# New fixed orders of four engines in the first part of an adaLN, linear-attention and MLP kernel

## The chip, the cores and the metric

The kernel runs on one core of a Trainium2 chip. The metric is the device time of one execution in microseconds (us). The program is written in the Tile layer of the chip's kernel language: a planner places tiles and semaphores, and each engine runs its own queue of instructions in order. The engines are named as in the profile: PE (TensorE, matrix products; its weight loads are shown as PEld), DVE (VectorE), ACT (ScalarE), POOL (GpSimd) and SP (SyncE, whose queue issues nearly all DMA transfers).

## What is computed

x is 2048 x 576, all float32. Six vectors of length 576 (sa, ca, ga, sb, cb, gb) come from the condition c.

```
mod = silu(c) @ w_mod, cut into sa, ca, ga, sb, cb, gb
h = layernorm(x) * (1 + ca) + sa
q, k, v = split(h @ wqkv)                  # 32 heads of 18
pq, pk = phi(q), phi(k)                    # phi(t) = (t + 1 if t > 0 else exp(t)) + 1e-6
kv = sum over s of pk v;  z = sum over s of pk
o = (pq kv) / (pq z + 1e-6)
x = x + ga * (o @ wo)
h = layernorm(x) * (1 + cb) + sb
x = x + gb * (silu(h @ w1) @ w2)           # w1: 576 x 4608, w2: 4608 x 576
```

## The kernel before

Every product is made of three passes: each float32 operand is split into a high part and a low remainder in the matrix unit's rounded float32 form (fp32r), and high by high, high by low and low by high are summed in psum. The high part is a cast, mostly on ACT (`split_h` L201, `w_hi` L294, the fetch of MLP weights L921 and L969); the low part is a subtraction, mostly on DVE (L117, and `w_lo` L299/L301).

The work has three parts.

1. *The front and attention* (0 to about 350 us). LayerNorm statistics (`stats` L174/175, `finish` L179 to L181, `normalise` L187/189), the modulation vectors (`add_mod`, `col_mod` L346, products with w_mod by L496/L498 on DVE from raw loads L263), transposes, and then k, v, kv and z for each of 16 tiles of 128 rows; later q, num and den, and the product with wo (`attn_out`, whose last step L737 adds a psum result to the residual tile `acc`, on DVE). At the very start PE runs products of ones by ones (`warm_up`, L395), 8 and then 10 in number, each two records of PE in the profile. The raw tiles of wqkv are loaded into parts of the `acc` tiles, which hold the residual later.
2. *The first MLP block beside attention* (from about 215 us). While the last tiles of attention are worked, a first group of the MLP is computed with its own tiles: `mlp_up` (L797, silu L799), `mlp_down` (L808 into the psum buffer `big`, added to `acc` by L813). The normalised tokens h of the second LayerNorm are transposed and stored to DRAM (`hd`, stores L873) on SP.
3. *The MLP* (from about 390 us to the end). Seven products of a Strassen-like scheme, with h streamed from `hd` (fetch L987/L991). `Unit.up` (L1233) and `Unit.down` (L1306) are PE's products; DVE adds the results (L1252, L1314). Weights come by `Weights.load1` (w1: a main transfer of 512 KB at L953 and two tails of 64 KB at L955) and `Weights.load2` (w2: 576 KB at L962) into tiles `v`. A w2 tile is multiplied by gb first (L918: one operation on DVE, two halves on POOL), sums of w1 pieces are made on POOL (L936 to L948), and a tail is cast to `wtb` on ACT (L921) with its low part on DVE (L117).

Two tiles `v` of the third part are the ones that held attention's merged matrix (`big<-v` of L222 on PE, one of attention's last products), so their first loads wait until PE has read it for the last time.

What sets the order: PE runs in the order of the program's text. For DVE, ACT, POOL and SP the first part and the second have fixed orders that are written out by hand: `ORDERS` (L55 to L99) holds for each engine a permutation of the numbers of its instructions (DVE 545, ACT 373, POOL 127, SP 109), and `arrange` makes each instruction follow the one listed before it on its engine. From the third MLP unit on, all engines run in program order. An instruction that waits holds up everything behind it on its engine.

Of the kernel before, what the change touches and what calls it, by code (L numbers as in the profile page):

```python
# [22 lines left out]
def kernel(ctx: ExitStack, tc, A_x, A_wqkv, A_wo, B_x, B_w1, B_w2, c, w_mod, out):  # L23
# [28 lines left out]
    def f32(ap):  # L52
# [1 line left out]

    ORDERS = {  # L55
        "DVE": """
            4 1 0 3 2 5-7 13 8 14 12 10 15 9 11 16-21 25-26 31 27 32 28 33-34 22-23 35 24 41-44 30 29 39 36-38 45-46
            40 47 50 48-49 62-63 65 51-52 56 66 84 64 57 53 55 58 61 85 59 86 80 60 88 81 87 67 83 68 82 69 71 70 72
            148 73-74 89 75-77 149 91 78 90 79 150 92 151 54 93 97 94 98 96 152 100 153 99 95 101-105 107 106
            108-109 111 110 125-126 128-129 127 131 130 132 134 133 135-137 112 138-139 113 141 140 114-115 142  # L60
            116-124 143-147 182-183 154 184-185 158 155 186 159 187 156 160 223 161-162 157 224-225 222 163 226 165
            164 166-171 173 172 192-193 195-196 194 197-199 201-202 200 203-204 174 205 208 175 209 176-177 206-207
            178-180 188 181 189-191 210-214 216 215 217-218 220 219 221 227-228 230-231 229 232-248 250-251 249
            252-254 256-258 255 259 261 263 260 265-266 262 264 269-271 275 268 276 267 277 273 272 274 300 282-284
            278-279 291-293 280 299 303-305 285 312-313 301 286-287 281 288 302 289 314 294 290 322 295-296 323
            297-298 324 306 331-332 307-310 315 333 341 311 316-319 342 320 325 343 321 353-354 326-329 334 355 330
            365 335 366 336-337 367 374 338 375 346 339 344-345 351 347 340 348-349 376 352 357-358 350 359-361 356
            385 362 386 363-364 387 368 404-405 369-371 406 372 423 373 377-378 424 379-380 383 382 381 391 388 390
            425 393 432 394-395 398 400 397 384 433 409-410 396 411-413 392 414 420 434 389 401 421 403 426 415 422
            399 427-428 431 417 402 416 407 429 418-419 430 435 408 436-437 440 438 441 444 504 439 442-443 446-450  # L70
            445 451 454 452-453 456-460 455 462 461 463 472 475 465 464 479 466 476 474 467 480 478 473 484 468-469
            481 471 486-487 470 482 492 494 493 495 489 488 496 483 497-498 490 499 502 477 491 500 485 503 501 520
            516 508 538 505 507 506 519 511 510 509 515 514 512-513 517-518 521 524 522-523 527 537 525-526 530-531
            529 532-535 528 536 539-544
        """,
        "Activation": """
            0-2 4-5 8 6-7 12 9 13 10-11 22 14 17 19 21 23-25 15-16 18 26-27 29 3 20 35 30 28 37-38 31 33 32 55-56
            58-59 36 39 57 42 44 40 45 41 43 50 53 51 34 54 52 60 46 48 47 61 49 62 64-67 63 69 68 70-74 76-77 75 78
            81 79 82 80 83 94-95 92 84 93 85-91 96-100 103-104 101 105 108 106 109 107 102 110-113 115-116 114 117
            120 118 121 119 122 131 133 123 134 124 132 125-130 135-138 140-141 139 142 145 143 146 144 147-149  # L80
            151-152 150 153 156 154 157 155 158-179 181 180 182-183 185 184 186-191 204 192-194 203 195 198 196-197
            205 199 202 200-201 206-207 210 208-209 219 216 213-214 212 218 211 217 215 220 223 221-222 224 226 228
            227 231 230 232 225 229 233-235 238 236-237 247 242 241 248 239 243 245 249-250 246 251 240 244 252-255
            259 261 257 260 256 262 264-265 263 273 267 266 258 269-270 278-279 268 282 280-281 277 275 274 276 283
            271-272 284-286 288 290-291 287 289 292 297-298 295 294 296 293 316 313 299 301-302 318 300 315 319-320
            317 303 305 304 307-308 314 309-310 306 311 322 312 323 328-329 325 324 321 330-331 326-327 333 332 334
            362 349 344 335-337 340 338 346 343 341 339 345 347 342 351 348 353 359 352 350 354 356 360 358 357 363
            361 365 364 355 366-370 372 371
        """,
        "Pool": """  # L90
            6 0 4 3 2 5 7-15 20 16-17 19 18 21-23 25 24 26 33 27 30 28 34 31-32 29 37 41 35-36 38-39 44 47 42-43 50
            45 40 54 46 48-49 57 51-52 60 84 55-56 53 72 58-59 76 61 79 62-64 73-74 67-68 77 65 78 71 66 69 75 80-81
            70 100 99 82-83 94 89-92 85-87 93 88 102 104 98 97 96 95 101 105-106 103 107-108 113 109-110 112 120 111
            114 117 122 115 119 118 123 121 124 116 125-127
        """,
        "SP": """
            0-26 28 27 29 36 30-31 37-40 45-47 32-35 48-51 53 52 54 41-44 61 60 59 55-57 62 58 63-67 70 68 71 69
            72-74 82 80 76-77 75 83 78 90 79 81 85 87 86 84 88 104 103 89 91 102 92 95 93 96 94 97-101 105 108
            106-107  # L99
        """,  # L100
    }

# [251 lines left out]
    def add_mod(k0, k1):  # L354

        o = sums[:, :, k0 * P : min(k1 * P, D)]
        V.scalar_tensor_tensor(o, mods[3][:, :, k0 * P : min(k1 * P, D)], sc[:, 3:4], o, op0=ALU.mult, op1=ALU.add)
        if k1 > KC:
            A.copy(sums[:, :, D:DX], sums[:, :, KC * P : D])

    def col_mod(k0, k1):
        for k in range(k0, k1):
            for a in range(2):
                mod_mm(sums[:, a], k, ones, a, last=True)
        V.tensor_add(cols["a"][:, k0:k1, :], mod_slots[k0 >= HEAD][:, :, :, 0],
                     plus1.unsqueeze(1).to_broadcast([P, k1 - k0, 2]))
# [17 lines left out]
    def k_part(tiles, passes, first=False, last=False):  # L384
        for n, (a, b) in enumerate(passes):
            for i in tiles:
                for h in range(2):
                    T.matmul(kps[i][:, h, :HALF], hT[0][:, a, i * P : i * P + P], wk_(b)[:, h * HALF : (h + 1) * HALF],
                             start=first and n == 0, stop=last and n == len(passes) - 1)
# [3 lines left out]
    def warm_up(n):  # L393
        for _ in range(n):
            T.matmul(warm_ps[:, 0, 0:P], ones, ones, start=True, stop=True)  # L395

    with tc.manual_schedule(engines={mybir.EngineType.PE}):
# [40 lines left out]
        def first_k(k):  # L438
            k_part(range(2), [(k, k), (KC + k, k)], k == 0)
# [6 lines left out]
        modulate(*args[1], A)  # L446
        add_mod(HEAD, KC + 1)
        ln.stats(2, xts[2])
        first_k(0)
        col_mod(HEAD, KC + 1)  # L450
        turn_tiles(pT, (0, 1), (KC,))
# [1050 lines left out]
```

## Time and profile before

| | us |
|---|---|
| median of 3 runs | 1165.44 |
| lowest and highest of them | 1164.58 and 1167.25 |
| the profiled execution, its own time | 1165.17 |
| its span in the trace | 1163.2 |
| PE busy | 1137.3 (98%) |
| DVE busy | 972.7 (84%) |
| POOL busy | 646.6 (56%) |
| ACT busy | 532.1 (46%) |

The span runs from the first to the last instruction in the trace; the execution's own time is 2.0 us longer. The mean granted clock of PE is 0.992 of full speed. The page of the profile sums the busy time by engine, cuts the span into 40 slices, follows back the chain of work that ended last and groups the instructions by line and operation. The trace answers further: a list of what each engine waited for, timelines of one engine, and windows (busy time of each engine in a stretch with the granted clock of PE and the share in which DMA was busy). An entry of a timeline is the start in us, the duration in us, the engine, the line, the operation, the tiles (out<-in) and the form; xN means N instructions in a row, and the bracket gives the idle time before and the instruction that ended it.

### The profile page before, as it was taken

The page shows a single profiled execution, that of the slowest core. Times are in us where ns is not written, and L with a number is a line of the kernel's source. Part 1 is how long each engine was busy: PE and PEld are TensorE (multiplying, and loading weights), DVE is VectorE, ACT ScalarE, POOL GpSimd, SP SyncE. Part 2 cuts the span into 40 slices and gives each one's busy share as a digit, 9 for nine tenths or more (in the row PEclk, how much of TensorE's full clock was granted, in tenths as well). Part 3 has the DMA queues.
Part 4 walks back from the last instruction along what each step waited for, and adds up shares of the span by engine and source line. Part 5 has one row for each costly group of instructions (what it writes and reads, how often), then busy time and mean ns, then how long its engine had stood idle before and what let it go on. Part 6 is the DMA issues. An engine that isn't in the chain of part 4 may idle for free.

```text
span 1163.2 us, 19621 instructions
## 1 busy us (share of the span) xinstructions
PE 1137.3 (98%) x7239; PEld 1058.0 (91%) x7239; DVE 972.7 (84%) x1552; ACT 532.1 (46%) x1087; POOL 646.6 (56%) x742
## 2 busy tenths in 40 slices
PE   8999999999996899999999999999999999999998
PEld 7999999899995799999999999999999999999998
DVE  5975643587767889999999999999999999999996
ACT  4643442436554444444454454444444444444541
POOL 1100000353624477677767757767766776776686
PEclk8999999999998999999999999999999999999999
DMA  9522100123238869769779788797697797697784
GB/s 291 149 80 76 43 1 1 47 69 122 65 123 314 292 263 348 277 259 366 270 266 351 263 304 321 259 339 294 252 352 278 258 349 278 257 365 266 265 309 153
DMA packets 57231, 268.62 MB, mean 231 GB/s; under 512 B 5484, under 2 KB 19312, under 8 KB 34096
## 3 DMA queue, kind: packets, MB, share of 16 engines
q1 hardware_dynamic: 57124, 267.36, 62.9%
q8 instruction: 58, 0.95, 0.3%
q14 instruction: 37, 0.30, 0.1%
q10 hardware_dynamic: 12, 0.00, 0.0%
HBM read 250.56 MB, written 16.78 MB: 230 GB/s over the span
## 4 chain that ended last, share of the span: by engine, by line
PE 93%; DMA 2%; DVE 2%; ACT 1%; issue 1%; POOL 0%; SPq 0%; DVEq 0%; ACTq 0%; POOLq 0%
PE up L1233 33%; PE down L1306 31%; PE psK L222 13%; PE big L222 7%; PE kvp L547 2%; PE big L808 2%; PE small L797 1%; DMA acc<-in_A_wqkv_dram 1%; PE big L723 1%; PE small L210 1%; DMA hT<-in_w_mod_dram 1%; DVE hT L117 1%; PE psT L210 1%; PE up L1336 1%; PE down L1336 1%; PE psK L691 1%
## 5 line engine op out<-in xcount | busy, mean ns | idle before, releaser
L1314 DVE TENSOR_TENSOR acc<-down,acc 128x576 f32<-128x576 f32 x330 | 246.1, 753 | 14.2 <-PE down L1306 5.2
L1233 PE MATMUL up<-hT,w 128*128 128x512 f32 x916 | 239.4, 390 | 0.8 <-DVE f L1252 0.8
L1233 PEld LDWEIGHTS up<-hT,w 128*128 128x128 f32 x916 | 164.5, 188 | 25.8 <-DVE f L1252 1.2
L1268 POOL TENSOR_TENSOR s<-f,f 128x256 f32<-128x256 f32 x66 | 51.8, 784 | 158.8 <-ACT f L1249 158.7
L1306 PE MATMUL down<-w,hb 128*128 128x288 f32 x792 | 120.8, 294 | 0.0
L1306 PE MATMUL down<-w,hc 128*128 128x288 f32 x792 | 120.6, 294 | 0.0
L1306 PEld LDWEIGHTS down<-w,hb 128*128 128x128 f32 x792 | 113.8, 188 | 5.3 <-DVE hb L1287 0.2
L1306 PEld LDWEIGHTS down<-w,hc 128*128 128x128 f32 x792 | 113.8, 188 | 5.1
L1314 DVE TENSOR_TENSOR U<-down,U 128x576 f32<-128x576 f32 x132 | 99.5, 754 | 17.4 <-PE down L1306 15.3
L117 DVE TENSOR_TENSOR w<-v,w 128x288 fp32r<-128x288 f32 (+1 forms) x170 | 113.2, 675 | 1.0 <-ACT w L977 0.9
L222 PE MATMUL psK<-w,hT 128*128 128x288 f32 (+2 forms) x660 | 107.8, 298 | 0.0
L222 PEld LDWEIGHTS psK<-w,hT 128*128 128x128 f32 x660 | 94.9, 189 | 0.3 <-DVE a L315 0.2
L1233 PE MATMUL up<-room,w 128*128 128x512 f32 x348 | 91.1, 390 | 0.0
L1287 POOL TENSOR_TENSOR hc<-s,hc 128x512 fp32r<-128x512 f32 x66 | 89.2, 1351 | 1.5 <-ACT hc L1283 1.5
L1249 ACT ACTIVATE f<-f 128x512 f32<-128x512 f32 x102 | 64.4, 632 | 47.9 <-DVE f L1254 25.5
L1252 DVE TENSOR_TENSOR f<-up,p 128x512 f32<-128x512 f32 x102 | 69.7, 683 | 14.0 <-PE up L1233 12.1
L180 POOL TENSOR_TENSOR rstd<-ve,neghalf 128x4 f32<-128x4 f32 (+3 forms) x10 | 9.7, 966 | 120.7 <-DVE ve L179 110.7
L1233 PEld LDWEIGHTS up<-room,w 128*128 128x128 f32 x348 | 62.5, 188 | 9.6 <-DMA room<-hd 0.2
L1272 POOL TENSOR_TENSOR f<-f,s 128x256 f32<-128x256 f32 x66 | 50.7, 768 | 36.9 <-DVE hb L1287 26.2
L977 ACT CAST w<-v 128x288 fp32r<-128x288 f32 x85 | 36.7, 434 | 74.6 <-PE down L1306 61.6
L1306 PE MATMUL down<-w,ha 128*128 128x288 f32 x396 | 63.0, 294 | 0.0
L1306 PE MATMUL down<-w,hd 128*128 128x288 f32 x396 | 62.9, 294 | 0.0
(285 smaller groups left out, 2534.8 us busy)
## 6 DMA issues: line engine op xcount, KB each, us to landing
hT<-hd SPq DMA_DIRECT2D x66, 1280.0 KB, 5.9
hT<-hd SPq DMA_DIRECT2D x45, 1024.0 KB, 5.6
room<-hd SPq DMA_DIRECT2D x35, 1280.0 KB, 5.9
room<-hd SPq DMA_DIRECT2D x20, 1024.0 KB, 5.0
v<-in_B_w_dram SPq DMA_DIRECT2D x17, 576.0 KB, 6.5
v<-in_B_w_dram SPq DMA_DIRECT2D x17, 512.0 KB, 8.4
hd<-S SPq DMA_DIRECT2D x6, 1024.0 KB, 8.3
xt<-in_A_x_dram SPq DMA_DIRECT2D x16, 288.0 KB, 4.6
```

What stands on the lines that cost most here:

```text
L117: return V.tensor_sub(lo, full, f32(hi))
L210: T.transpose(ps[:, i * P : (i + 1) * P], xt[i][:, cidx * P : (cidx + 1) * P], ident)
L222: T.matmul(ps, xpart(a), wpart(b), start=n == 0, stop=n == len(XW) - 1)
L977: A.copy(self.w2[n][:, 0], src)
L1233: T.matmul(ps, left, right, start=first and m == 0, stop=m == len(seq) - 1, skip_group_check=True)
L1249: A.activation(self.f[i, k], self.f[i, k], AF.Silu)
L1252: V.tensor_add(f, self.bank[bank[1]], self.p1)
L1268: G.tensor_add(self.s[:, 0:1], half(i, 0, 1), half(i, 1, 1))
L1272: G.tensor_sub(half(i, 1, 0), half(i, 1, 0), self.s[:, 1:2])
L1287: eng.tensor_sub(t[:, :, 1, :], src, f32(t[:, :, 0, :]))
L1306: T.matmul(ps[:, p, :HALF], self.a[i, n][:, u, p * P : (p + 1) * P], self.w.w2[n][:, v], start=n in (1, 5, 7, 6) and j == 0, stop=j == 2, ...
L1314: V.tensor_add(dst, ps[:, :, :HALF], dst)
```

## The change

Two things are changed. First, all four lists in `ORDERS` are new permutations of the same numbers. Second, one line is added: `warm_up(8)`, eight more products of ones by ones, 16 records of PE, behind the statistics of the third token tile and ahead of the first products with wk. The rest of PE's order is unchanged. Since the new lists take three lines fewer and the call one more, lines behind L443 have a number smaller by two in the kernel after, and those ahead of it by three.

What moves, by the lines of the code before:

- ACT at the start: before w cast 0 (L294), w cast 1, h of the first half tile (L201), L195, a normalise, h of the second, w 2, w 3, w 4, three normalises, L195, h of the third and fourth, three more w casts, a load of the activation table with one small operation (L414), h of the fifth. After: w 0, h of the first, L195, w 1, h of the second, the table load with its operation, w 2, w 3, a normalise, w 4, three normalises, a cast of wv, L195, h of the third, then the other casts and h in turn.
- SP near 350 us: before, the load of w2 (L962, number 90) stood ahead of stores of h (L873, numbers 79 and 81) and of the loads of w1 (L955 and L953, numbers 85 to 87). After: the stores first (79, 78, 81, 84), then the two tails (87, 86), the main part (85), then L962 (90).
- DVE near 350 us: before, L918 (number 504) stood ahead of two of the last three additions of attention (L737, the first of them number 446). After: it stands behind all of them, behind the normalise of the last tile (L189) and behind the low part of `wtb` and of the first w pieces. The low part of `wtb` (number 472) stands ahead of the last normalise.
- POOL near 350 us: the two halves of L918 (numbers 100 and 99) stood ahead of the sums of w1; after, they stand behind them.
- Elsewhere neighbours change places on DVE, ACT and POOL, among them the L498 products with the later pieces of w_mod between 45 and 62 us.

The diff, cut to its core:

```diff
     ORDERS = {
         "DVE": """
...
-            445 451 454 452-453 456-460 455 462 461 463 472 475 465 464 479 466 476 474 467 480 478 473 484 468-469
+            440 442 444 441 443 446-447 439 448-449 454 450 455 451-453 445 456-459 464 460 472 463 461 478 462 504
...
-            425 393 432 394-395 398 400 397 384 433 409-410 396 411-413 392 414 420 434 389 401 421 403 426 415 422
-            399 427-428 431 417 402 416 407 429 418-419 430 435 408 436-437 440 438 441 444 504 439 442-443 446-450
...
         "Activation": """
-            0-2 4-5 8 6-7 12 9 13 10-11 22 14 17 19 21 23-25 15-16 18 26-27 29 3 20 35 30 28 37-38 31 33 32 55-56
+            0-2 4 6 8 7 5 12 9-11 13-14 3 17 19 22 21 24-25 23 26 15-16 29 18 27 35 20 55 31 56 28 57 30 33 32 37 36
...
         "Pool": """
...
-            70 100 99 82-83 94 89-92 85-87 93 88 102 104 98 97 96 95 101 105-106 103 107-108 113 109-110 112 120 111
+            75 66 70 80-82 94 83 89-90 85 91-92 86-87 93 100 88 99 102 98 104 101 105-106 96-97 103 107 95 108-111
...
         "SP": """
-            0-26 28 27 29 36 30-31 37-40 45-47 32-35 48-51 53 52 54 41-44 61 60 59 55-57 62 58 63-67 70 68 71 69
-            72-74 82 80 76-77 75 83 78 90 79 81 85 87 86 84 88 104 103 89 91 102 92 95 93 96 94 97-101 105 108
-            106-107
+            0-25 27-28 26 36 29-31 37-40 45-47 32-35 48-54 41-44 60 59 61 55-58 62-67 70 68-69 71-73 80 76 74 82 77
+            75 83 79 78 81 84 87 86 85 90 89 103 88 91 104 92 95 93 96 94 97-102 108 105-107
         """,
     }
...
         modulate(*args[1], A)
         add_mod(HEAD, KC + 1)
         ln.stats(2, xts[2])
+        warm_up(8)
         first_k(0)
```

More of the change, by code (lines that the diff above doesn't have):

```diff
@@ L56 @@
         "DVE": """
[L57 to L66, printed above, removed]
@@ L67 @@
-            365 335 366 336-337 367 374 338 375 346 339 344-345 351 347 340 348-349 376 352 357-358 350 359-361 356
-            385 362 386 363-364 387 368 404-405 369-371 406 372 423 373 377-378 424 379-380 383 382 381 391 388 390
-            425 393 432 394-395 398 400 397 384 433 409-410 396 411-413 392 414 420 434 389 401 421 403 426 415 422
-            399 427-428 431 417 402 416 407 429 418-419 430 435 408 436-437 440 438 441 444 504 439 442-443 446-450
-            445 451 454 452-453 456-460 455 462 461 463 472 475 465 464 479 466 476 474 467 480 478 473 484 468-469
@@ L72 @@
-            481 471 486-487 470 482 492 494 493 495 489 488 496 483 497-498 490 499 502 477 491 500 485 503 501 520
-            516 508 538 505 507 506 519 511 510 509 515 514 512-513 517-518 521 524 522-523 527 537 525-526 530-531
-            529 532-535 528 536 539-544
+            0 4-5 1-2 6-7 13-14 10 8 15-16 11-12 9 17-18 3 19-21 25-27 31 28 22 32 23 41 33 24 34-35 43 30 45 44 42
+            29 39 36-37 46 38 50 40 47 84 48-49 51 62 56 52 85 57 63 86 58 87 59 64 60 65 53 80 55 66 148 81 54 67
@@ new lines @@
+            88 68 82 69 71 70 72 61 73-74 83 89 75-76 78 149 77 79 91 90 150 93 151 96 94 97 152-153 98 92 99-100 95
+            101 103 102 104-109 111 110 125-126 128 127 129 131 130 132 134-135 133 136-137 112 138-139 141-142
+            113-114 140 115-123 143 124 144-147 154 182-184 155-156 185 158 157 159 186-187 160 162 161 222 225
+            223-224 163 226 164-167 169 168 170-171 173 172 192-196 198 197 199 201-202 200 203-204 174 205-206 208
+            207 175-177 209 178-180 188 181 189-191 210-214 216 215 217-218 220 219 221 227-228 230 229 231-258 261
@@ new lines @@
+            263 265 262 266 264 259-260 269-271 275 268 276 267 277 272-274 300 278-279 282-283 280 284 291-293
+            303-304 299 281 285-286 305 312-313 287-289 301 294 290 314 322-323 295-297 324 298 331 306-309 332 310
+            302 333 341-342 315-319 343 320 325 321 353 326-328 311 354 329 334 355 365 330 335-336 366 337-339 345
+            367 340 374 346 375 344 347-349 351 350 376 385 352 386 356-363 387 404-405 364 368-371 373 406 372
+            423-424 377-380 383 382 381 425 391 432 388 390 433 393-394 397 392 400 395-396 398 384 434 410-413 409
@@ new lines @@
+            420 414 401 415 389 421 416 418 426 417 422 402 427-428 431 403 407 429 399 419 430 408 436 435 437-438
+            440 442 444 441 443 446-447 439 448-449 454 450 455 451-453 445 456-459 464 460 472 463 461 478 462 504
+            465 475 467 480 466 469 484 471 481 468 487 486 470 473 482 494 492 495 493 488-489 496 483 474 497 491
+            498-500 490 501-502 477 479 476 485 538 503 505 508 507 506 510 516 511 519 512 515 509 513-514 520 517
+            524 518 521 527 522-523 537 525-526 530-531 529 536 533-534 532 535 539 528 541-544 540
@@ L75 @@
         """,
         "Activation": """
-            0-2 4-5 8 6-7 12 9 13 10-11 22 14 17 19 21 23-25 15-16 18 26-27 29 3 20 35 30 28 37-38 31 33 32 55-56
-            58-59 36 39 57 42 44 40 45 41 43 50 53 51 34 54 52 60 46 48 47 61 49 62 64-67 63 69 68 70-74 76-77 75 78
-            81 79 82 80 83 94-95 92 84 93 85-91 96-100 103-104 101 105 108 106 109 107 102 110-113 115-116 114 117
-            120 118 121 119 122 131 133 123 134 124 132 125-130 135-138 140-141 139 142 145 143 146 144 147-149
@@ L81 @@
[L81 to L85, printed above, removed]
@@ L86 @@
-            317 303 305 304 307-308 314 309-310 306 311 322 312 323 328-329 325 324 321 330-331 326-327 333 332 334
-            362 349 344 335-337 340 338 346 343 341 339 345 347 342 351 348 353 359 352 350 354 356 360 358 357 363
-            361 365 364 355 366-370 372 371
+            0-2 4 6 8 7 5 12 9-11 13-14 3 17 19 22 21 24-25 23 26 15-16 29 18 27 35 20 55 31 56 28 57 30 33 32 37 36
+            38 58-59 39-40 42 41 43-45 50-51 34 53 52 54 60 48 46 49 61 47 62 64-66 63 67 69-70 68 71-74 76-77 75 78
@@ new lines @@
+            81 79 82 80 83 94 92 84 93 95 85-91 96-101 103-104 102 105 108 106 109 107 110-113 115-116 114 117 120
+            118 121 119 122 133 131 123 134 132 124-130 135-138 140-141 139 142 145 143 146 144 147-149 151-152 150
+            153 156 154 157 155 158-179 181 180 182-183 185 184 186-191 204 192-194 203 195 198 196-197 199 202
+            200-201 205-207 210 208-209 219 213 216 215 218 211 214 217 212 220 223 221-222 224 226 225 227 230-232
+            228-229 233-236 238 237 247 239 241 245 243 246 248 244 249 251 250 240 242 252-255 259 261-263 260 257
@@ L89 @@
+            256 264-265 267 273 266 258 269 268 278 270 279 275-276 274 282 280-281 277 271-272 283-287 290-291 288
+            292 289 297-298 293 296 294-295 313 299 316 319 301 317-318 300 314 302-303 305 304 306-307 309 308 310
+            320 311-312 322 315 323 328-329 324-325 330-331 321 326-327 332-334 362 335-336 349 344 337 340 338 341
+            343 342 339 346 345 347 351-352 348 353 350 354 360 356-357 359 355 358 363 361 364-370 372 371
         """,
         "Pool": """
-            6 0 4 3 2 5 7-15 20 16-17 19 18 21-23 25 24 26 33 27 30 28 34 31-32 29 37 41 35-36 38-39 44 47 42-43 50
@@ L92 @@
-            45 40 54 46 48-49 57 51-52 60 84 55-56 53 72 58-59 76 61 79 62-64 73-74 67-68 77 65 78 71 66 69 75 80-81
-            70 100 99 82-83 94 89-92 85-87 93 88 102 104 98 97 96 95 101 105-106 103 107-108 113 109-110 112 120 111
-            114 117 122 115 119 118 123 121 124 116 125-127
+            6 0 4 3 7-8 2 5 9-10 12 11 13-15 20 16-17 19 18 21-25 33 26-27 30 28 34 31 37 29 32 41 35-36 38 44 47 39
+            42 50 43 45-46 40 54 48-49 57 51-52 84 60 55-56 72 53 58-59 76 61-62 79 63 73 64 67-68 74 77 71 65 69 78
@@ L95 @@
+            75 66 70 80-82 94 83 89-90 85 91-92 86-87 93 100 88 99 102 98 104 101 105-106 96-97 103 107 95 108-111
+            113 112 114 117 120 122 115 123 118-119 124 116 121 125-127
         """,
         "SP": """
-            0-26 28 27 29 36 30-31 37-40 45-47 32-35 48-51 53 52 54 41-44 61 60 59 55-57 62 58 63-67 70 68 71 69
-            72-74 82 80 76-77 75 83 78 90 79 81 85 87 86 84 88 104 103 89 91 102 92 95 93 96 94 97-101 105 108
-            106-107
+            0-25 27-28 26 36 29-31 37-40 45-47 32-35 48-54 41-44 60 59 61 55-58 62-67 70 68-69 71-73 80 76 74 82 77
```

## The prediction, made before the result was known

> **What bounds the kernel now.** I read the page first, then TensorE's list of waits, then the timelines of the engines that the largest waits name, and last the windows for the granted clock. Lines of code are those of the kernel before.
>
> ```profile
> span 1163.2 us, 19621 instructions
> ## 1 busy us (share of the span) xinstructions
> PE 1137.3 (98%) x7239; PEld 1058.0 (91%) x7239; DVE 972.7 (84%) x1552; ACT 532.1 (46%) x1087; POOL 646.6 (56%) x742
> ```
>
> TensorE (PE) is busy for 1137.3 of 1163.2 us. The change gives it the same products and 16 records more, so orders can win only from the 1163.2 − 1137.3 = 25.9 us in which it is idle and from stretches in which its clock is low. The list of PE's waits (engine, line, whom it waited for: total us, times, longest) says where the idle time lies:
>
> ```profile
> PE big L808 <- DVE acc L737: 8.7, 1, 8.7
> PE psK L388 <- ACT hT L201: 4.1, 1, 4.1
> PE small L797 <- DVE hT L117: 1.9, 2, 1.0
> PE small L210 <- ACT sl L799: 1.3, 1, 1.3
> ```
>
> Two single waits are half of it: 8.7 us before a first-down product of the MLP (L808), 4.1 us before the first products with wk (L388). Both lie in the part whose orders are written out. The first, on PE's timeline (start us, us, operation; in brackets the idle time ahead and its releaser):
>
> ```profile
> 342.79 1.83 PE L808 MATMUL big<-w,hs 128*128 128x288 f32 x12
> ...
> 356.95 3.22 PE L808 MATMUL big<-w,hs 128*128 128x288 f32 x12 [8.70 <-DVE acc L737]
> ...
> 392.70 1.55 PE L1233 MATMUL up<-first,w 128*128 128x512 f32 x6
> ```
>
> PE stopped at 356.95 − 8.70 = 348.25 because a psum buffer was free only after VectorE (DVE) had added it to acc (L737). DVE's timeline shows why the add was late:
>
> ```profile
> 352.86 0.76 DVE L918 TENSOR_TENSOR v<-v,bc_gb 128x576 f32<-128x576 f32 x1 [12.59 <-DMA v<-in_B_w_dram]
> ...
> 356.05 0.76 DVE L737 TENSOR_TENSOR acc<-big,acc 128x576 f32<-128x576 f32 x1
> ...
> 363.84 0.57 DVE L189 TENSOR_SCALAR xn<-acc,mv,rstd 128x576 f32<-128x576 f32 x1
> 364.33 0.41 DVE L117 TENSOR_TENSOR wtb<-v,wtb 64x256 fp32r<-64x256 f32 x1
> ```
>
> DVE stood from 352.86 − 12.59 = 340.27 at L918, which scales a w2 tile by gb; the add was queued behind it. The tile's load is on the sync queue (SP):
>
> ```profile
> 348.28 0.38 SPq L962 DMA_DIRECT2D v<-in_B_w_dram  x1
> 348.76 0.89 SPq L873 DMA_DIRECT2D hd<-S  x2
> 349.70 1.48 SPq L953 DMA_DIRECT2D v<-in_B_w_dram  x1
> ```
>
> SP could issue it only at 348.28: its room, a v tile, had been read by attention's last products until then (PE stops at 348.25). So PE waited for DVE, DVE for a load, and the load for PE. It is an order that makes the hole, not a lack of any engine.
>
> **The change, part by part.**
>
> *DVE's L918 and SP's L962 (the large term).* In the new DVE list L918 (index 504) stands behind all three last adds L737 (before: ahead of the last two) and behind LayerNorm's last normalise. On SP the h stores (L873) now come first, then the w1 loads L955 and L953, then L962. Nothing that L737 needs is then later than 348.25: its attention products stand ahead of 348.25 on PE, and DVE has been idle since 340.27. So the wait of 8.70 us goes: **−8.7**.
>
> What is late next? For L918 itself nothing: its tile feeds the down products, which follow the first up product at 392.70, while a load issued a few us behind 348.25 lands within ten (the longest row below), so some 30 us cover it. POOL's two halves of L918 move back with it, and the w1 sums on POOL forward; both feed units behind 392.70. Late can be wtb, the small w1 tail. In the new list its DVE operation (L117, 0.41) stands ahead of the last normalise (L189, 0.57), and it waits for a load L955. From issue to landing the v loads and, on quieter queues, the x loads took (us min, median, max; then KB and median):
>
> ```profile
> DMA to landing us min/median/max: 4.2/7.0/9.8
> ```
>
> ```profile
> acc<-in_A_x_dram SPq DMA_DIRECT2D x12, 288.0 KB, 2.8
> ```
>
> The load goes out right behind the stores, about 349.0 (348.25 and two issues of 0.4). It lands at 351.8 with 2.8, at 353.2, 356.0 or 358.8 with 4.2, 7.0, 9.8. Add a cast on ScalarE (ACT), which I price as the DVE operation, 0.41, then 0.41 and 0.57: xn is ready at 353.2, 354.6, 357.4 or 360.2. Before, xn was ready at 363.84 + 0.57 = 364.41, which is 7.46 us behind the start of L808 and includes some 1.6 us of low clock (next part); the same place is now 348.25 + 7.46 − 1.6 = 354.1. So the cost is 0, 0.5, 3.3 or 6.1 us. I take 0, near the first two: at 348.28 a load of 576 KB, nine times the size of a tail (64 KB in the code), was there at 352.86, 4.6 us later, and the tails now go out before the large ones. The other ends stay in the range.
>
> The small waits behind it (1.9 on hT, 1.3 on sl in the list) I cost at no change: the chains of ACT and DVE that end in them begin with the same products, which all move forward together. Bounds: −3.2 (both go) to the +6.1 above.
>
> *The clock behind the hole.* Windows (PE, PEld, DVE, ACT, POOL busy; granted clock; DMA share; GB/s):
>
> ```profile
> 357.00:360.00 3.00, 3.00 (x13) 3.00 (x14) 2.18 (x7) 0.36 (x2) 1.16 (x1) 0.50 0.65 221
> 20.00:22.00 2.00, 2.00 (x9) 2.00 (x10) 2.00 (x4) 2.00 (x5) 0.00 (x0) 0.50 1.01 351
> ```
>
> After the hole PE works for 3 us at a granted 0.50. The twelve L808 products took 3.22 there and 1.83 at 342.79: 1.39 lost, and the first L797 behind them loses a little more, at most another 0.3. Without a hole there is no reason for the low clock: **−1.6** (bounds −1.4 and −1.7). The Trainium skill, "TensorE: Matmul & The Clock Gate", section "Part 1: The HAM clock gate", says that an idle window of about 3.4 us halves TensorE's clock and a busy one restores it. The rows agree: 8.70 us idle, then 0.50.
>
> *The front: ACT's first h ahead of w, and the 8 products of ones.* PE's timeline, then ACT's:
>
> ```profile
> 5.17 2.62 PE L395 MATMUL psK<-ones 128*128 128x128 f32 x20
> ...
> 19.86 2.29 PE L388 MATMUL psK<-w,hT 128*128 128x288 f32 x8 [4.09 <-ACT hT L201]
> ...
> 26.76 1.30 PE L388 MATMUL psK<-w,hT 128*128 128x288 f32 x8
> ...
> 32.90 0.53 PE L222 MATMUL psK<-w,hT 128*128 128x256 f32 x2
> ```
>
> ```profile
> 17.72 0.67 ACT L294 CAST w<-acc 128x576 fp32r<-128x576 f32 x1 [2.03 <-DMA acc<-in_A_wqkv_dram]
> ...
> 25.46 0.41 ACT L201 CAST hT<-raw 128x256 fp32r<-128x256 f32 x1
> ...
> 28.26 1.28 ACT L414 ACT_TABLE_LOAD   x1
> ```
>
> PE is idle from 15.77 to 19.86, then works at half clock (0.50 in 20 to 22) until about 26. The 16 new records cost 16 × 2.62/20 = 2.1 us at full clock, twice that, 4.2, at half. They stand in the idle 4.09 us, so full-clock products end at 17.9 and add nothing. The w cast at 17.72 waits for its load in both orders (2.03), and with the first h directly behind it (before: another w cast between, 0.67, and a wait for that chunk) L388 can begin at about 18.7, 1.1 earlier. At full clock the first stretch is then over earlier still: but the third group of products, at 26.76, needs the third h (ACT L201, 25.46) and its low half on DVE. ACT's new list puts the table load (1.28 + the small operation behind it, 0.2) and one more w cast (0.67) ahead of that h, 2.1 us, against waits for chunks of about 1.1 that the new list fills and the 0.4 us it now has in hand: I work the chain through and get the third h ready between 0 and 0.3 us later than before. What comes back: the table load no longer stands between this h and the later ones that PE waits for just ahead of 32.90. In all **−0.4** at 32.90. Bounds: were all of the half-clock stretch, 19.86 to 26.76, on the path, half of 6.9, −3.4; were the clock to fall once more behind it, +3.4. I take −0.4, near 0, because ACT had no gap longer than a few tenths from 18 to 30, so the group at 26.76 is bound by ACT and the loads, not by PE's clock.
>
> *The rest (33 to 340 us)*: the new lists swap neighbours on DVE, ACT and POOL, and PE's products keep their order. In one of the fullest places:
>
> ```profile
> 44.00:48.00 4.00, 4.00 (x32) 4.00 (x32) 3.97 (x13) 0.68 (x2) 0.31 (x1) 1.00 0.87 233
> 49.65 1.41 DVE L498 SCALAR_TENSOR_TENSOR tmod<-raw,sc,tmod 128x1152 f32<-128x1152 f32 x1
> ```
>
> ```profile
> raw<-in_w_mod_dram SPq DMA_DIRECT2D x6, 576.0 KB, 4.3
> ```
>
> PE is busy for all of 4.00 us there, so there is nothing to win, and DVE for 3.97, so there may be something to lose (below). I cost it at 0; all waits of this stretch in PE's list are 1.1 us or less each.
>
> **The sum**: 1165.17 (the profiled execution, 2.0 above its span and 0.3 below the median 1165.44) − 8.7 − 1.6 − 0.4 = **1154.5 us**, with all else at 0.
>
> **The rivals.**
>
> *A, the forecast*, 1151.5 to 1157: chance **0.65**.
>
> *B, the wait moves to the load of wtb.* DVE stands at wtb with the last normalise behind it, exactly as it stood at L918. For it: a landing of 7.0 us is the median of this tile's loads, and the large loads go out 1 to 2 us later on the same queues. Against it: the tail is small and first. With 7.0 to 9.8 it costs 3.3 to 6.1: **1157.8 to 1160.6**. Chance 0.12.
>
> *C, the clock falls again in the front.* PE, at full clock, is through its first products sooner and waits for the third h, with only transposes between; a drop of the length seen, 6.9 us, loses 3.4: **1158.3** (0.4 less if the front's gain stands). For it: the fall after 4.09 us. Against it: its work in between is several short groups, no single gap need reach 3 us. The Trainium skill, "TensorE: Matmul & The Clock Gate", section "Part 4: PE-mode transpose", states that transposes do not count as a busy TensorE in the way products do, which would favour this case; no row here separates the two. Chance 0.06.
>
> *D, more goes than the hole.* The waits behind it (1.9 + 1.3) go too, or the front keeps the clock's 3.4: 1151.3 or **1151.5**. Against it: those waits end ACT and DVE chains, not stalls in a list. Chance 0.07.
>
> *E, slower: DVE waits for w_mod in the attention stage.* Between 45 and 62 us four L498 (1.41 each) stand in DVE's list among the operations that free PE's psum buffers. In the new list some of them stand earlier, and each waits for a raw load of 4.3 us; if each waits in full, 4 × 4.3 = 17.2 and DVE, 3.97 of 4.00 busy, has no slack to take it back: **1171.7**. It decides as soon as more than 10.7 + 2.3 = 13 us of such waits reach PE. For it: DVE is the full engine there. Against it: SP issues these loads in nearly the same order in both lists. Chance 0.07.
>
> *F, the change does not act*: the stall stays, because the last L737 depends on something I have not seen: **1165**. Chance 0.03.
>
> **How the numbers follow.** The predicted time is A's, 1154.5. The range takes in A, D, B and C: D's lower end with a little of both its gains, 1150.5, to B's end, 1161; E and F stay out (0.10). Faster by over 0.2% (2.3 us, about what a measurement of this kernel tells from no change) is A, B, C and D, 0.90; within 0.2% is F, 0.03; slower is E, 0.07.
>
> **What would show it.** Right: no wait of PE for L737 near 348; L808 of that place taking 1.83 or so, at a clock of 1.0; L918 on DVE behind the last normalise; the first up product near 382, 10 us before 392.70; v_proj's first product (32.90) between 32 and 33. Wrong: a wait of 3 us or more of PE for xn (B); windows at 0.50 between 26 and 33 (C); new PE waits for DVE between 45 and 62 (E); a PE wait for L737 that has only another releaser (F).

## The result, and the profile after

| | runs | median us | lowest to highest | ratio to before, 95% interval |
|---|---|---|---|---|
| before | 4 | 1165.32 | 1164.58 to 1167.25 | |
| after | 4 | 1156.13 | 1154.94 to 1156.63 | 0.9917 (0.9900 to 0.9934) |

The changed kernel takes 9.7 us less by the ratio (7.7 to 11.7 by its interval); 10.7 less was forecast. The sum is right to about a microsecond, and part of that is luck: the front and the middle cost 4.2 us more than forecast, and small waits behind the hole gave 2.2 us that the sum put at nothing. The profiled execution of after took 1156.63 us. Lines of the kernel after are smaller by 3 up to L443 and by 2 behind it: L806 is L808 of before, L735 is L737, L916 is L918, L385 is L388, L219 is L222.

The head of its page, and the first rows of PE's list of waits:

```profile
span 1154.7 us, 19658 instructions
## 1 busy us (share of the span) xinstructions
PE 1137.1 (98%) x7255; PEld 1057.1 (92%) x7255; DVE 977.0 (85%) x1552; ACT 532.1 (46%) x1087; POOL 649.3 (56%) x742
```

```profile
PE kvp L343 <- DMA hT<-in_w_mod_dram: 1.8, 1, 1.8
PE big L806 <- DVE hs L114: 1.6, 2, 1.0
PE psT L368 <- ACT xt L184: 1.6, 1, 1.6
```

The wait of 8.7 us for the accumulation is not in the list any more; what is left is small. PE's busy time is as before (1137.1 against 1137.3), 17.6 us of the span are idle instead of 25.9. Three waits are new: for w_mod (the first product behind the second group of ones), for `hs` (L806) and for `xt` (L368). PE's timeline, in the front and at the former hole:

```profile
28.12 1.99 PE L385 MATMUL psK<-w,hT 128*128 128x288 f32 x8 [0.80 <-ACT hT L198]
29.91 2.39 PE L385 MATMUL psK<-v,hT 128*128 128x288 f32 x10
...
35.16 0.53 PE L219 MATMUL psK<-w,hT 128*128 128x256 f32 x2
```

```profile
352.08 1.76 PE L806 MATMUL big<-w,hs 128*128 128x288 f32 x12
353.68 1.53 PE L795 MATMUL small<-hT,w 128*128 128x512 f32 x6
...
385.88 2.89 PE L1231 MATMUL up<-first,w 128*128 128x512 f32 x12
```

The twelve L806 follow attention without a gap and take 1.76 us, where they took 3.22. Set beside the rows of before, the same places of PE's program give the account:

| place on PE | before | after | difference |
|---|---|---|---|
| first product of v | 32.90 | 35.16 | +2.26 |
| attention's last product is over | 348.25 | 352.08 | +3.83 |
| the down products behind it begin | 356.95 | 352.08 | −4.87 |
| the next products (L797) | 359.97 | 353.68 | −6.29 |
| first up product of the third part | 392.70 | 385.88 | −6.82 |
| span | 1163.2 | 1154.7 | −8.5 |

So the front lost 2.3 us and the stretch from there to the end of attention (33 to 348 before) another 1.6; the hole gave 8.7 and the clock 1.4; behind it 0.5 and then 1.7 were gained. DVE at the hole (one stretch of its timeline), and SP:

```profile
352.28 0.76 DVE L735 TENSOR_TENSOR acc<-big,acc 128x576 f32<-128x576 f32 x1 [0.48 <-PE big L219]
...
356.40 0.42 DVE L114 TENSOR_TENSOR wtb<-v,wtb 64x256 fp32r<-64x256 f32 x1 [1.58 <-ACT wtb L919]
356.75 0.57 DVE L186 TENSOR_SCALAR xn<-acc,mv,rstd 128x576 f32<-128x576 f32 x1
...
360.42 1.89 DVE L916 TENSOR_TENSOR v<-v,bc_gb 128x576 f32<-128x576 f32 x1
```

```profile
352.27 1.58 SPq L953 DMA_DIRECT2D v<-in_B_w_dram  x2
353.91 0.58 SPq L951 DMA_DIRECT2D v<-in_B_w_dram  x1
354.53 0.51 SPq L960 DMA_DIRECT2D v<-in_B_w_dram  x1
```

DVE waits for PE at L735 now, not PE for DVE; L916 stands behind the last normalise. The two tails go out first, at 352.27, and their low part on DVE starts 4.1 us later with 1.58 us of waiting.

### The profile page after: what moved, and what is told of

The parts are those of the page before. It is cut to its first block, busy times and chain, and to the rows that moved or that the text cites. A ratio compares the mean times of both kernels' runs of the same rounds, so it can differ in the third digit from the quotient of the medians.

```text
span 1154.7 us, 19658 instructions
## 1 busy us (share of the span) xinstructions
PE 1137.1 (98%) x7255; PEld 1057.1 (92%) x7255; DVE 977.0 (85%) x1552; ACT 532.1 (46%) x1087; POOL 649.3 (56%) x742
## 4 chain that ended last, share of the span: by engine, by line
PE 92%; DVE 2%; ACT 2%; DMA 1%; SPq 1%; issue 0%; POOL 0%; POOLq 0%; ACTq 0%; DVEq 0%
PE up L1231 33%; PE down L1304 32%; PE psK L219 13%; PE big L219 6%; PE kvp L545 2%; PE big L806 2%; DMA hT<-in_w_mod_dram 1%; PE psK L689 1%; PE psK L385 1%; PE big L721 1%; PE small L207 1%; PE psT L207 1%; PE up L1334 1%; PE small L795 1%; PE down L1334 1%
## 5 line engine op out<-in xcount | busy, mean ns | idle before, releaser
L114 DVE TENSOR_TENSOR w<-v,w 128x288 fp32r<-128x288 f32 (+1 forms) x170 | 116.6, 695 | 3.6 <-ACT w L967 3.5
L219 PE MATMUL psK<-w,hT 128*128 128x288 f32 (+2 forms) x660 | 107.7, 298 | 0.0
L219 PEld LDWEIGHTS psK<-w,hT 128*128 128x128 f32 x660 | 94.9, 189 | 0.3 <-DVE a L312 0.2
L1270 POOL TENSOR_TENSOR f<-f,s 128x256 f32<-128x256 f32 x66 | 51.0, 772 | 35.2 <-DVE hb L1285 24.7
```

Source lines behind the costliest of these rows:

```text
L114: return V.tensor_sub(lo, full, f32(hi))
L219: T.matmul(ps, xpart(a), wpart(b), start=n == 0, stop=n == len(XW) - 1)
L1270: G.tensor_sub(half(i, 1, 0), half(i, 1, 0), self.s[:, 1:2])
```

## The experiments

All ratios are to runs of the kernel before on the same chip. In the kernels made from before the lines are those of before; where products of ones are added or the lists end a line earlier, they shift by one.

| kernel | runs | median us | ratio, 95% interval |
|---|---|---|---|
| l918_only | 11 | 1163.76 | 0.9987 (0.9978 to 0.9996) |
| l918_both | 11 | 1166.05 | 1.0008 (1.0000 to 1.0017) |
| three_queues | 11 | 1163.36 | 0.9991 (0.9982 to 1.0001) |
| no_sp | 6 | 1173.35 | 1.0076 (1.0062 to 1.0090) |
| late_all | 4 | 1152.08 | 0.9893 (0.9880 to 0.9906) |
| old_front | 6 | 1155.99 | 0.9926 (0.9914 to 0.9938) |
| new_old_new | 4 | 1152.62 | 0.9895 (0.9883 to 0.9908) |
| new_front | 8 | 1167.47 | 1.0026 (1.0015 to 1.0036) |
| before_warm | 11 | 1164.47 | 1.0001 (0.9992 to 1.0010) |
| after_nowarm | 4 | 1154.87 | 0.9915 (0.9902 to 0.9928) |
| after_nowarm2 | 5 | 1154.34 | 0.9912 (0.9899 to 0.9925) |
| after_again | 5 | 1156.44 | 0.9930 (0.9918 to 0.9943) |

### The hole: what has to move for it to go

**l918_only**, one number moved on DVE:

```diff
-  ... 441 444 504 439 442-443 446-450 ... 461 463 472 475 ...
+  ... 441 444 439 442-443 446-450 ... 461 463 472 504 475 ...
```

> The kernel before with one number moved: L918 (504) on DVE behind the last normalise and the low part of wtb; SP, ACT and POOL keep their old lists, so SP still loads w2 first and the w1 tail last. Theory 1 (L918's place on DVE is the whole cause of the hole): PE's wait for L737 near 348 goes and the clock stays at 1.0, 8.7 + 1.6 = 10.3 us less than before, about 1155. Rival (SP's order is needed too: the load of wtb comes last and something waits for it): a new PE wait of 3 to 6 us between 350 and 365, so 4 to 7 us less than before, 1158 to 1161.

It gained 1.5 us (0.5 to 2.6), where theory 1 gave 10.3. The wait for L737 did go, and PE then waited for `hT` (4.0 us at 356.85) and for xn. PE's list, DVE's timeline and POOL's:

```profile
PE small L797 <- DVE hT L117: 5.9, 3, 4.0
```

```profile
356.03 0.16 DVE L181 SCALAR_TENSOR_TENSOR nm<-mv,rstd 128x3 f32<-128x3 f32 x1 [10.73 <-POOL rstd L180]
```

```profile
353.64 1.54 POOL L918 TENSOR_TENSOR v<-v,bc_gb 128x288 f32<-128x288 f32 x2 [25.49 <-DMA v<-in_B_w_dram]
355.14 0.85 POOL L180 TENSOR_TENSOR rstd<-ve,neghalf 128x3 f32<-128x3 f32 x1
```

POOL's own halves of L918 had been waiting for the same load since 328, and the rstd of LayerNorm's last tiles stood behind them. In the trace of before this second lock could not be seen: DVE's was opened by the same load. Theory 1 falls. The rival has a new wait of the size that it gave, but named the wrong cause: it looked for the load of wtb.

**l918_both** moves POOL's halves as well:

```diff
-  ... 75 80-81 70 100 99 82-83 94 89-92 85-87 93 88 102 ...
+  ... 75 80-81 70 82-83 94 89-92 85-87 93 100 88 99 102 ...
```

> The kernel before with three numbers moved: L918 on DVE (504) as in the run before, and its two halves on POOL (100 and 99) behind the w1 sums; SP's list stays old. Theory 1, as the run before changed it (the w2 tile is waited for on two queues, DVE's and POOL's, and both must be moved): PE waits neither for L737 nor for xn behind POOL's rstd, 10 to 12 us less than before, 1153 to 1155. Rival (SP's order is a third lock: the w1 tail is loaded last, and ACT's casts of it hold up sl and xn): a new wait of 3 to 6 us by ACT or wtb, 1157 to 1161.

Nothing gained. PE passed the old hole and then waited 7.9 us for `sl`. PE's list and ACT's timeline:

```profile
PE small L797 <- ACT sl L799: 7.9, 1, 7.9
```

```profile
358.48 0.40 ACT L969 CAST w<-v 128x256 fp32r<-128x256 f32 x1 [11.61 <-DMA v<-in_B_w_dram]
358.81 0.40 ACT L921 CAST wtb<-v 128x256 fp32r<-128x256 f32 x1
359.12 0.59 ACT L799 ACTIVATE sl<-small 128x512 f32<-128x512 f32 x1
```

ACT stood for 11.61 us at a cast of the main w1 load, and `sl` was the second instruction behind it. In the new list L921 alone stands ahead of `sl`, and the L969 casts behind.

**three_queues** adds SP's new order to that, **no_sp** adds ACT's in its place:

```diff
 SP of three_queues:
-  ... 83 78 90 79 81 85 87 86 84 88 104 103 89 91 102 ...
+  ... 83 78 79 81 84 87 86 85 90 89 103 88 91 104 92 ...
 ACT of no_sp:
-  ... 293 316 313 299 301-302 318 300 315 319-320 ...
+  ... 313 299 316 319 301 317-318 300 314 302-303 ...
```

> L918 moved on DVE and POOL as before, and SP's new list behind 335 us: stores of h first, then the w1 tails, the main w1 load, w2 last. ACT keeps its old list, where the cast of the main w1 load (L969) stands ahead of sl. If SP's order is the last lock: 10 to 12 us less than before, about 1153. If ACT's cast is a lock of its own: the main load, issued near 350, lands 4 to 8 us later, and PE waits for sl 2 to 6 us: 1156 to 1160, 0.993 to 0.996 of before.

> L918 moved on DVE and POOL, and ACT's new list behind 335 us (only the cast of the w1 tail, L921, ahead of sl, the main casts behind it); SP keeps its old list, with w2, two stores and the main w1 load ahead of the tail. If ACT's order was the lock that held the run with DVE and POOL alone: 10 to 12 us less than before, about 1153. If SP's is one too: the tail, issued near 350 behind all the others, lands 5 to 9 us later, sl waits for it nearly as long as before: 1158 to 1164.

three_queues: 1.0 us less (2.1 less to 0.1 more). The rival for ACT came true (3.4 us for `sl`), and was not all. PE's list, and ACT 50 us later:

```profile
PE small L797 <- ACT sl L799: 3.4, 1, 3.4
PE small L797 <- DVE hT L117: 3.1, 2, 2.2
PE up L1233 <- ACT p L1208: 3.0, 1, 3.0
```

```profile
410.11 0.41 ACT L969 CAST w<-v 128x256 fp32r<-128x256 f32 x1 [6.84 <-DMA v<-in_B_w_dram]
410.42 0.58 ACT L1208 COPY p<-up 128x512 f32<-128x512 f32 x1
```

SP's new list issues the second main w1 load behind a fetch of h, at 401.46, where the old one did at 374.27; ACT's old list still has its cast ahead of `p`. So the new SP list opens a wait unless ACT's goes with it.

no_sp is 8.9 us slower than before (7.2 to 10.5), outside what either theory gave. ACT's first wait moved from the main load to the tail, which SP's old list issues behind all others:

```profile
360.10 0.41 ACT L921 CAST wtb<-v 128x256 fp32r<-128x256 f32 x1 [11.29 <-DMA v<-in_B_w_dram]
```

```profile
PE small L797 <- ACT sl L799: 7.3, 1, 7.3
PE big L808 <- DVE hs L117: 4.8, 1, 4.8
```

The new ACT list with DVE's and POOL's old lists (but for L918) made a second wait, for `hs` at 376: DVE's list has a low part of w ahead of that `hs`, and it waited 6.6 us for a cast that the new ACT list has later. SP's new order cannot stand alone: a store that it puts ahead of L962 needs h from behind L918 on DVE, and L918 would wait for L962, a circle.

**late_all** takes all four new lists from 335 us on and the old ones ahead of it, with no new products of ones:

```diff
 DVE, the seam:
-  ... 435 408 436-437 440 438 441 444 504 439 442-443 446-450 445 451 454 452-453 ...
+  ... 435 408 436-438 440 442 444 441 443 446-447 439 448-449 454 450 455 451-453 ...
 ACT, the seam:
-  ... 271-272 284-286 288 290-291 287 289 292 297-298 295 294 296 293 316 313 ...
+  ... 271-272 284-287 290-291 288 292 289 297-298 293 296 294-295 313 299 316 ...
```

> Old lists for all that ran before 335 us in the trace of before, the new lists behind it, no new products of ones. By the two traces PE gained 11.1 us between 348 and 365 and 1.3 behind that, and lost 4.0 ahead of it. Theory 1 (the stages are independent): 12.4 us less than before, about 1153, that is 3 to 4 less than the changed kernel. Rival (what the changed kernel has behind 348 came with the later start of its first part, or the loss ahead is noise of one execution): as the changed kernel, 1156.

12.5 us less (10.9 to 14.0), as theory 1 said. `sl` costs PE 0.9 us here. DVE, POOL and ACT waited for the same few loads, each with work behind it that PE needed, and SP's order set which load came first. Changing one, two or three of these lists gave between 1.5 us of gain and 8.9 of loss, all four together 12.5. late_all takes every other exchange behind 335 us too: whether the moves named here, L918 on two queues with SP's and ACT's new orders, would give the 12.5 by themselves was not run.

### The front and the middle

**old_front** is the changed kernel with the old lists up to 33 us and no new products of ones; **new_front** has the new ones, with the products of ones, up to 35.2 us and the old lists behind; **new_old_new** has the new lists up to v's first product and from 335 us, the old ones between, and no products of ones. All are cut as late_all is, by start times in a trace. ACT's list at its head, the seam in its second half:

```diff
 old_front, against after:
-  0-2 4 6 8 7 5 12 9-11 13-14 3 17 19 22 21 24-25 23 26 15-16 29 18 27 35 20 55 31 56 28 ...
+  0-2 4-5 8 6-7 12 9 13 10-11 22 14 17 19 21 23-25 15-16 18 26-27 29 3 20 35 30 28 ...
 new_front, against before:
-  0-2 4-5 8 6-7 12 9 13 10-11 22 14 17 19 21 ... 29 3 20 35 30 28 37-38 31 33 32 55-56 ...
+  0-2 4 6 8 7 5 12 9-11 13-14 3 17 19 22 21 ... 35 20 55 31 56 28 57 30 37-38 33 32 58-59 ...
 new_old_new, against late_all:
-  0-2 4-5 8 6-7 12 9 13 10-11 22 14 17 19 21 ... 29 3 20 35 30 28 37-38 31 33 32 55-56 ...
+  0-2 4 6 8 7 5 12 9-11 13-14 3 17 19 22 21 ... 35 20 55 31 56 28 57 30 33 37-38 32 58-59 ...
```

> Old lists for all that ran before 33 us in the trace of before (v's first product), no new products of ones, the new lists behind. Theory 1 (the new front costs the 2.3 us that the traces show at v's first product): 2.3 us less than the changed kernel, about 1153.8. Rival (the 2.3 us are an early DMA wait of that one execution, or are taken back later): as the changed kernel, 1156.

> The new lists for all that ran before 35.2 us in the trace of the changed kernel, with the eight products of ones, and the old lists behind. If the new front costs what the traces show at v's first product: 2 us more than before, 1167. Rival (this was chance): as before, 1165. Rival, the forecast: 0.4 less.

> The new lists ahead of v's first product, without the products of ones; the old lists from there to 335 us; the new ones behind. If the three stretches are independent: 1.1 less than late_all by the front (29.44 against 30.57 in the traces), 1 to 3 less than the changed kernel without the products of ones, about 1151 and the fastest of all. Rival: as late_all or worse, 1152 to 1153, because the new front hands on its tiles in another order than the old middle wants (as the old front did to the new middle, 1.2 us at its seam).

new_front costs 3.0 us (1.7 to 4.2), so the front's loss is real; its trace has the first product of v at 34.27, 1.4 us behind the 32.90 of before, with PE's waits for `xt` 1.6 and for h 1.1 as in after. Its span is 2.6 us longer than that of before; the other 1.2 arise behind the first up product, and why stays open. old_front was not 2.3 us faster than after: PE was there at the old time, but the seam cost 1.2 us (a wait of L222 for DVE's L315), and the middle then lost what it loses in after. new_old_new equals late_all within the intervals, so a new front without products of ones brings nothing that can be measured.

The middle's 1.6 us can be read in the traces: from v's first product to the end of attention PE takes 315.2 to 315.5 us with the old middle (before, before_warm, new_front, late_all, new_old_new) and 316.9 to 317.2 with the new one (after, after_again, after_nowarm, after_nowarm2). Where they come from, on PE in before, on PE in after, and on ACT in after:

```profile
296.79 1.75 PE L808 MATMUL big<-w,hs 128*128 128x288 f32 x12
298.38 0.71 PE L723 MATMUL big<-ident,pn 128*128 128x128 f32 x5
```

```profile
298.93 1.21 PE L806 MATMUL big<-w,hs 128*128 128x288 f32 x5
301.13 1.20 PE L806 MATMUL big<-w,hs 128*128 128x288 f32 x7 [0.99 <-DVE hs L114]
302.17 0.71 PE L721 MATMUL big<-ident,pn 128*128 128x128 f32 x5
```

```profile
296.60 0.60 ACT L798 CAST hs<-sl 128x512 fp32r<-128x512 f32 x1
297.11 0.87 ACT L184 ACTIVATE xn<-acc,nm,rstd 128x576 f32<-128x576 f32 x1
297.88 0.57 ACT L797 ACTIVATE sl<-small 128x512 f32<-128x512 f32 x1
298.36 0.68 ACT L723 CAST qT<-big 128x640 fp32r<-128x640 f32 x1
298.93 0.62 ACT L798 CAST hs<-sl 128x512 fp32r<-128x512 f32 x1
```

The new ACT list puts a normalise (0.87) and the cast of qT (0.68) between the first `hs` and the second, and PE waits for it in the middle of the twelve L806. Ahead of them after lies 2.1 us behind before, and 3.8 behind them: the whole 1.6 arises there. The old list has the second `hs` ahead of both, and PE has no such wait there.

**before_warm** is before with the one new line; **after_nowarm** and **after_nowarm2** are after without it; **after_again** is after.

```diff
         ln.stats(2, xts[2])
+        warm_up(8)
         first_k(0)
```

> The kernel before with the eight products of ones and nothing else. If the group at 26 us is bound by ACT's h: within 0.5 us of before. Rival (the clock, once up, saves PE time on the path): 1 to 3 us less. Rival (the clock falls later, at a group that is on the path): 1 to 2 us more.

> The changed kernel without the eight products of ones. If the group of products at 28 us is bound by ACT's h and not by PE's clock: within 0.5 us of the changed kernel, with the clock at 0.5 in 20 to 26 again. Rival (the clock that they keep up is worth something): up to 2 us more. Rival (they only bring the fall of the clock to a worse place, 0.64 in 29 to 33): 1 to 2 us less.

> The changed kernel without the eight products of ones, again. If these products cost 1 to 2 us with the new lists, by the clock that then falls at 28 us instead of 18: ratio to before 0.9905 to 0.992, against 0.9917 and 0.9930 of the changed kernel. If they cost nothing: 0.992 to 0.993.

> The changed kernel once more, beside the others on one chip. If v's first product is 2.3 us late by the lists: as in its first profile, about 35 us, and 0.9917 of before. If that is an early wait for w_mod of one execution: about 33 us in this profile and a time up to 2 us less.

With the old lists the products change nothing (1.0001, 0.9992 to 1.0010). With the new ones the intervals overlap (0.9917 and 0.9930 with, 0.9915 and 0.9912 without), but of nine times without them (median 1154.76) eight lie below the third lowest of the nine with them (median 1156.38): some 1.6 us, a hint rather than a verdict, since the runs are of different chips. The traces say more: v's first product comes at 31.3 to 33.1 us in the eleven that lack the new front or the new products of ones, and at 34.3 to 35.2 in the three that have both (new_front, after, after_again). Neither shows a cost there by itself; the two together do. The windows of after_again, then of before_warm:

```profile
22.00:25.00 3.00, 0.79 (x4) 0.56 (x4) 2.59 (x5) 2.97 (x6) 0.00 (x0) 1.00 1.06 259
25.00:28.00 3.00, 1.92 (x9) 1.68 (x10) 2.80 (x7) 2.97 (x7) 0.00 (x0) 0.67 1.04 317
28.00:31.00 3.00, 3.00 (x15) 3.00 (x14) 2.59 (x5) 2.61 (x6) 0.82 (x1) 0.50 1.06 263
31.00:34.00 3.00, 3.00 (x18) 3.00 (x18) 0.00 (x0) 0.52 (x1) 0.96 (x1) 0.69 0.88 260
```

```profile
22.00:25.00 3.00, 2.24 (x16) 1.68 (x15) 1.82 (x5) 2.56 (x5) 0.00 (x0) 1.00 1.05 287
25.00:28.00 3.00, 2.42 (x17) 2.18 (x18) 2.23 (x5) 2.79 (x7) 0.00 (x0) 1.00 1.04 284
28.00:31.00 3.00, 1.88 (x14) 1.65 (x14) 1.49 (x3) 2.98 (x6) 0.00 (x0) 1.00 1.05 273
```

In after_again PE runs its first products at full clock, is then busy for 2.7 of 6 us, and the clock falls just when 28 products are ready in a row: 3.00 us busy at 0.50. In before_warm PE is busy for 4.7 of the same 6 us and the clock stays at 1.00. Without the products, in after_nowarm, the low clock lies at 19 to 25, on work behind which PE waits for ACT in any case (0.62 us at 26.22):

```profile
19.00:22.00 3.00, 3.00 (x15) 3.00 (x15) 0.91 (x3) 2.97 (x6) 0.57 (x1) 0.50 1.03 346
22.00:25.00 3.00, 3.00 (x14) 2.80 (x14) 2.58 (x6) 2.97 (x6) 0.00 (x0) 0.50 1.05 304
25.00:28.00 3.00, 2.38 (x17) 2.14 (x17) 2.81 (x7) 2.97 (x8) 0.00 (x0) 0.97 1.00 283
```

after_again also settles the early wait for w_mod: the 1.8 us of the first profile are not in it, and v's first product is late all the same, at 34.98. The two profiles come to nearly the same place by different ways. In the first the third group of products (26.76 before) begins 1.4 us late, at 28.12, behind that wait, and the low clock adds 0.9; in after_again it begins on time, at 26.73, and the low clock adds all of the 2.1.

## Why the prediction was right, and where it was not

- **The hole, −8.7: right in size, incomplete in cause.** All 8.70 went. The prediction said that it was DVE's order and SP's load. l918_only and l918_both show that these were the first of four locks. POOL's move was priced at nothing, "both feed units behind 392.70", and ACT's part near 350 was not looked at beyond one cast; in the whole change both are indeed free, but without them there is no gain.
- **The clock behind the hole, −1.6: right.** L806 took 1.76 us against 3.22, 1.46 less, and the window 351 to 354 has a granted clock of 1.00.
- **The wait for wtb (rival B): did not come.** DVE waited 1.58 us for it at 356.40, and xn was ready at 357.32, 5.2 us behind the start of L806, where 5.9 cost nothing. The step that took 0 was right.
- **The small waits, 0: too little.** 0.5 us went by the first up product and 1.7 behind it, against −3.2 as the bound. Two waits of the third part that the prediction did not count went nearly whole. PE's list of before, then of after:

```profile
PE up L1233 <- DVE f L1252: 0.8, 1, 0.8
...
PE up L1233 <- DVE acc L813: 0.5, 1, 0.5
```

```profile
PE up L1231 <- DVE f L1250: 0.2, 1, 0.2
```

- **The front, −0.4: wrong; rival C came true.** The step that failed is the clause that the group at 26.76 "is bound by ACT and the loads, not by PE's clock". For that group it was nearly right: in after_again its start is at 26.73. But its 8 products and the 20 behind them run without waiting and are bound by the clock, and with the new front the products of ones move the low clock onto them. v's first product came 2.3 us late in after and 2.1 in after_again. C's price was 3.4 for 6.9 us at half clock: by the windows the half clock lasted 6.8 us in after_again, part of it while PE waited, and 3.4 us in after (0.58 in 28 to 31, 0.85 in 31 to 34), where the late start behind the wait for w_mod made up the rest. C had a chance of 0.06, with "no single gap need reach 3 us" against it. No gap did (the longest is 1.6 us), and the clock fell.
- **33 to 348 us, 0: wrong by 1.6.** The term was put at nothing because no wait in the stretch was over 1.1 us and PE kept its order; a new wait was looked for on DVE alone. The place was not DVE between 45 and 62 (rival E: PE's list has no wait there) but ACT at 297 to 299.

In the two profiled executions (1165.17 and 1156.63) that makes −10.3 forecast for hole and clock against −10.1 found; −0.4 against +3.8 ahead of the hole; 0 against −2.2 behind it. Of the signs that the prediction named for being right, the first three came; v's first product (35.16, not 32 to 33) and the first up product (385.88, not 382) did not.

## What to carry to other kernels

When queues are in fixed order and one load is late, look at every engine's first instruction that waits for it, not only at the one that the profile names: the last lock to open hides the others, and changing one list of four moved the wait and gave 1.5 us of 12.5. The loads, the casts and the operations that use them must change places together, so an order is to be tested as a whole stretch, cut at a time at which it is closed. late_all, which leaves the change's front and middle out, is with new_old_new the fastest kernel of these: 1152.08 us, 0.9893 of before, where the whole change has 0.9917 and 0.9930.

## What the runs showed of the hardware that was not expected

The granted clock fell without a long idle gap: in after_again it fell at about 26.0 (0.54 in the window 26.0 to 26.5), when PE had been busy for 1.37 of 3 us and its longest wait was 1.6 us. With 1.68 of the same 3 us (before_warm) it stayed at 1.00. The Trainium skill, "TensorE: Matmul & The Clock Gate", section "Part 1: The HAM clock gate", speaks of an idle window of about 3.4 us; here a stretch that was less than half busy was enough. Its section "Part 4: PE-mode transpose", by which transposes do not count as busy, is not tested by these runs: the four transposes in that stretch take 0.66 us, and without them PE has no products from 23.7 to 26.7, 3.0 us. But after_nowarm2 shows the fall without transposes ahead of it. These are its windows; PE had been idle for 1.7 us, since 17.11, when the clock fell near 18.8:

```profile
15.80:18.80 3.00, 1.16 (x8) 0.97 (x8) 3.00 (x10) 1.01 (x3) 0.00 (x0) 1.00 1.07 309
18.50:19.00 0.50, 0.00 (x0) 0.00 (x0) 0.50 (x2) 0.24 (x1) 0.00 (x0) 0.85 1.06 217
```

A thin stretch does not always bring the fall: in new_old_new PE is busy for 0.80 of the 3 us from 24.0 to 27.0, and the clock stays at 1.00. What decides between them these runs do not show.

Products of ones that fill an idle stretch are therefore no free gain: they keep the clock up across it, and if the work behind them is thin, the fall can come later, onto work that is not.
